# Attention loads of a fused attention and mixture-of-experts kernel tied to TensorE's position, with the strided values stored in 80 rows

## The chip, the cores and the metric

The kernel runs on one core of one Trainium2 chip. TensorE (PE), VectorE (DVE), ScalarE (ACT), GpSimd (POOL) and SyncE (SP) each work through their own instruction queue. Direct loads of this kernel are issued from SP's queue, indirect ones from POOL's, and all of them run on the core's 16 DMA engines. The metric is device time in microseconds (us) of one execution; lower is better.

## The reference

The reference is an attention layer whose output goes, token by token, through one of eight experts. Cut to what matters:

```
B, H, S, D = 8, 8, 576, 64            # heads 0-3 look at a local window, heads 4-7 at every 32nd key
rel = pos[:, None] - pos[None, :]
local   = (rel >= 0) & (rel < 32)
strided = (rel >= 0) & (pos[None, :] % 32 == pos[:, None] % 32)
scores = where(mask, q @ k.T / sqrt(D), -1e9)
x = (softmax(scores) @ v)             # -> N = 4608 tokens of 512 numbers
logits = x @ w_gate + modality_bias[modality_id];  e = argmax(logits)
out[token] = softmax(logits)[e] * (relu(x @ w1[e]) @ w2[e])       # w1: 512x1024, w2: 1024x512 per expert
```

All is float32.

## The kernel before

**Two stages.** The first stage computes the attention in 32 units; the second runs the experts' two matrix products over slots of 256 tokens that belong to one expert. The second stage starts while the routing of the last tokens is still being finished.

**Units.** A unit is either `Local` (one local head of two batches) or `Strided` (a pair of strided heads of one batch). They alternate: units 0, 2, 4 and so on are local, units 1, 3, 5 and so on strided, 16 of each. Eight units make a group of two batches, after which `finish_pair` turns the group's outputs round, computes its routing and scatters its token rows into a buffer in memory (`xd`).

**What a unit loads.** All of it is issued from SP's queue.
- Queries and keys: two loads of 296 KB (local, into `lqk`) or 288 KB (strided, into `sqk`). One fills the even rows of the tile and one the odd rows. Each kind has two tiles, used in turn, so a tile is free again once the scores of the unit four places earlier are done.
- Values of a local unit (`vv`, two tiles): the first seven local units (`SPREAD = 7`) load 317 KB in four pieces, `vb` twice, `ve` and `vf`, and two POOL copies of about 1 us each then spread them (`spread_values`). The other nine load 585 KB in two pieces from `vl`, without copies.
- Values of a strided unit (`vs`, two tiles): one load of 72 rows of 4 KB, 288 KB.

**The loop.** Iteration n of the loop at the end of the first stage calls, in this order: the query and key load of unit n+3, the value load of unit n-1, for even n `spread_values` of unit n-2, the scores of unit n, `turn` of unit n-2 (transposes of its weights on TensorE), the masks of unit n+1, and the products with the values (`values`) of unit n-3. Between these stand pieces of `finish_pair` (`pop`, `slow`).

**Who sets the order.** TensorE's instructions stand in the order of the program in this stage (`manual_schedule`). The queues of the other engines, SP's among them, are ordered by the framework's scheduler, which works with a cost model, unless an instruction is held in program order by `pin`. A load waits for what it needs: that its tile is free, and that the direct load eight places before it has landed, as the direct loads share eight semaphores in turn. The function `paced` adds one more wait to an instruction: for the TensorE instruction that `recent` names, which is the one recorded last in program order. It is used before for the scatters of the routing, for the early fetches of weights and tokens, and for two small copies.

## Time and profile before

| | |
|---|---|
| median of three runs | 599.7 us (595.32 to 600.47) |
| the profiled execution | 597.48 us, span of its instructions 595.4 us |
| mean granted TensorE clock in it | 0.977 of full speed |
| TensorE matmuls busy | 564.8 us, 95% of the span |
| first stage | from the start to about 158 us, when the first matmul of an expert runs |
| bytes moved by DMA | 100.57 MB, mean 169 GB/s |

In the rows of the profile an arrow points from what is read to what is written (`o<-vv,et`), `xN` counts records, and a bracket `[1.64 <-issue]` gives the time that the engine sat idle before and what ended it; "issue" stands where the engine waited for nothing that the profile shows. `PEld` rows are TensorE's loads of its stationary operand. `SPq` and `POOLq` rows are issues of DMAs. A window row gives, for a stretch of time, the busy microseconds and the records of each engine, then the granted TensorE clock, the mean busy share of the DMA engines and the GB/s that they moved.

### The profile page before, as it was taken

Reading aid. Unit: us, or ns where it says so; the run is one execution under the profiler, and the core shown is the slowest. Engines: PE = TensorE matmul, PEld = TensorE weight load, DVE = VectorE, ACT = ScalarE, POOL = GpSimd, SP = SyncE. Lnnn points to the kernel's source line nnn. Section 1 sums busy time; section 2 is a strip of 40 time slices with the busy share of each in tenths; the row PEclk is TensorE's granted clock in tenths of the full one; section 3 lists DMA queues with packets and bytes.
Section 4 is the critical chain, followed back from the end, with each engine's and each line's share of the span. In section 5 each row is a group of like instructions: output and inputs, shape, how many; then the busy total and the mean of one; then the engine's idle time right before and its main releaser. Section 6 shows DMA issues by size and latency. Waiting matters only on the chain.

```text
span 595.4 us, 15277 instructions
## 1 busy us (share of the span) xinstructions
PE 564.8 (95%) x6040; PEld 494.4 (83%) x6040; DVE 426.1 (72%) x1050; ACT 358.7 (60%) x739; POOL 244.7 (41%) x219
## 2 busy tenths in 40 slices
PE   6979888989998999999999999999999999999995
PEld 3767776767887989999899899999998998998984
DVE  6776662957969997767767777777777677677541
ACT  3455664657866566666666666665665666666641
POOL 1413240143757786642543533533534533332220
PEclk9789997989999999999999999999999999999998
DMA  8988895897788855955934823413403438200621
GB/s 275 250 220 217 250 344 189 276 341 258 262 215 210 259 164 164 236 184 129 250 119 125 248 98 74 108 36 73 109 21 87 109 119 252 71 16 22 244 91 38
DMA packets 66669, 100.57 MB, mean 169 GB/s; under 512 B 47775, under 2 KB 49055, under 8 KB 63008
## 3 DMA queue, kind: packets, MB, share of 16 engines
q0 software_dynamic: 19744, 58.57, 29.7%
q1 hardware_dynamic: 46560, 40.56, 27.0%
q8 instruction: 49, 0.80, 0.6%
q10 hardware_dynamic: 288, 0.41, 0.2%
q14 instruction: 28, 0.23, 0.1%
HBM read 121.74 MB, written 19.43 MB: 237 GB/s over the span
## 4 chain that ended last, share of the span: by engine, by line
PE 85%; issue 5%; DVE 4%; DMA 3%; ACT 2%; POOL 1%; SPq 0%; POOLq 0%; ACTq 0%
PE h L924 33%; PE o L938 32%; PE o L420 3%; PE s L380 3%; PE ot L520 3%; PE lg L571 2%; PE xs L217 2%; PE t L217 2%; PE ss L476 1%; PE xl L217 1%; PE ts L217 1%; DMA vv<-in_vb 1%; ACT wh L959 1%; DVE wl L960 1%; DMA lqk<-in_qkl 1%
## 5 line engine op out<-in xcount | busy, mean ns | idle before, releaser
L960 DVE TENSOR_TENSOR wl<-raw,wh 128x512 fp32r<-128x512 f32 x288 | 185.9, 686 | 85.0 <-ACT wh L959 84.9
L959 ACT CAST wh<-raw 128x512 fp32r<-128x512 f32 x288 | 164.0, 618 | 91.4 <-PE o L938 89.6
L924 PE MATMUL h<-xl,wh 128*128 128x256 f32 x576 | 162.1, 282 | 1.4 <-DVE xl L912 1.4
L924 PE MATMUL h<-xh,wh 128*128 128x256 f32 x576 | 163.0, 284 | 0.2 <-ACT xh L911 0.2
L924 PE MATMUL h<-xh,wl 128*128 128x256 f32 x576 | 162.8, 283 | 0.0
L811 POOL DMA_INDIRECT raw<-in_w,wi x72 | 92.7, 1287 | 162.4 <-DVE wl L960 154.1
L924 PEld LDWEIGHTS h<-xl,wh 128*128 128x128 f32 x576 | 108.8, 189 | 8.1 <-DVE xl L912 2.1
L938 PE MATMUL o<-wh,hh 128*128 128x512 f32 x288 | 114.6, 398 | 0.0
L924 PEld LDWEIGHTS h<-xh,wh 128*128 128x128 f32 x576 | 108.4, 189 | 7.1 <-issue 0.6
L938 PE MATMUL o<-wl,hh 128*128 128x512 f32 x288 | 113.6, 395 | 0.0
L938 PE MATMUL o<-wh,hl 128*128 128x512 f32 x288 | 112.2, 395 | 0.0
L924 PEld LDWEIGHTS h<-xh,wl 128*128 128x128 f32 x576 | 108.3, 188 | 0.9
L927 ACT ACTIVATE hh<-h 128x256 fp32r<-128x256 f32 x144 | 55.2, 384 | 55.0 <-PE h L924 52.7
L929 DVE SCALAR_TENSOR_TENSOR hl<-h,hh 128x256 fp32r<-128x256 f32 x144 | 60.3, 419 | 12.5 <-ACT hh L927 12.3
L646 POOL DMA_INDIRECT xd<-xt,posi x36 | 40.4, 1121 | 59.1 <-DVE sms L496 16.5
L938 PEld LDWEIGHTS o<-wh,hl 128*128 128x128 f32 x288 | 53.7, 188 | 11.8
L938 PEld LDWEIGHTS o<-wh,hh 128*128 128x128 f32 x288 | 54.3, 188 | 7.6
L938 PEld LDWEIGHTS o<-wl,hh 128*128 128x128 f32 x288 | 54.3, 189 | 5.8
L946 POOL DMA_INDIRECT out<-y,le x36 | 46.2, 1283 | 24.0 <-ACT y L945 16.1
L792 POOL DMA_INDIRECT fx<-xd,li x36 | 39.2, 1090 | 23.6 <-issue 8.5
L409 ACT COPY et<-t 64x512 f32<-64x512 f32 x32 | 18.5, 579 | 21.1 <-PE t L217 20.7
L420 PEld LDWEIGHTS o<-vv,et 128*64 128x64 f32 x512 | 19.0, 152 | 13.4 <-issue 10.1
(183 smaller groups left out, 687.9 us busy)
## 6 DMA issues: line engine op xcount, KB each, us to landing
lqk<-in_qkl SPq DMA_DIRECT2D x32, 296.0 KB
sqk<-in_qks SPq DMA_DIRECT2D x32, 288.0 KB
vv<-in_vl SPq DMA_DIRECT2D x9, 520.0 KB
vs<-in_vs SPq DMA_DIRECT2D x16, 288.0 KB
raw<-in_w,wi POOLq DMA_INDIRECT x72, 2.5
vv<-in_vb SPq DMA_DIRECT2D x7, 146.2 KB
vv<-in_vb SPq DMA_DIRECT2D x7, 130.0 KB
vv<-in_vl SPq DMA_DIRECT2D x9, 65.0 KB
```

What stands on the lines that cost most here:

```text
L217: recent[:] = [nc.tensor.transpose(dst, src, ident)]
L420: recent[:] = [nc.tensor.matmul(os[bb][64 * jj:64 * jj + 64, bb + k, :], et[:, 2 * (k // 2) + bb, 2 * (k % 2) + jj, :, :].rearrange("p g q ...
L646: scattered(bp, paced(nc.gpsimd.indirect_dma_start(xd[0:(bp + 1) * T2, :], IOA(ap=posi[:, i:i + 1], axis=0), xt[:, i, :], None)))
L792: yield xt, fetches(min(xrows // T2, NBP) - 1, nc.gpsimd.indirect_dma_start(xt[:, h, :], None, xd[0:xrows, :], IOA(ap=li[:, s, h:h + 1], a ...
L811: return nc.gpsimd.indirect_dma_start(raws[j].rearrange("p f c -> p (f c)"), None, a["w"], IOA(ap=wi[:, s, j:j + 1], axis=0), bounds_check ...
L924: recent[:] = [nc.tensor.matmul(hp, w[:, a1], x[:, c, :], start=(k == 0), stop=(k == 11))]
L927: nc.scalar.activation(hh[:], hp, AF.Relu)
L929: nc.vector.scalar_tensor_tensor(hl[:], hp, 0.0, hh.bitcast(F32), ALU.max, ALU.subtract)
L938: nc.tensor.matmul(os[h], hx[:, m], w[:, 512:1024], start=(f == 0 and i == 0), stop=(f == 7 and i == 2))
L946: outs.add(nc.gpsimd.indirect_dma_start(out, IOA(ap=le[:, h, 0:1], axis=0), y[:], None, bounds_check=NT - 1, oob_is_err=False))
L959: nc.scalar.copy(wh[:, c], raw[:, c])
L960: nc.vector.tensor_tensor(wl[:, c], raw[:, c], wh[:, c].bitcast(F32), ALU.subtract)
```

## The change

Four things are changed.

1. `load` of a unit issues one of its two query and key loads, chosen by `x`, where it issued both.
2. In the loop, for n of 1 and more, the first of the two (`x` = 0) is called at the head of iteration n and the second after the scores of unit n. Both go through `paced`: the first waits for the last recorded TensorE instruction of iteration n-1, the second for the last matmul of the scores of unit n. For that, local scores now also set `recent`, in their last four matmuls.
3. The value load of unit n-1 is called after `turn` of unit n-2 in iteration n, and goes through `paced` too: it waits for the last transpose of that `turn`. The value loads of the first two local and the first two strided units are held in program order by `pin` as before; only unit 0's is still called ahead of the scores.
4. The values of a strided unit are stored in 80 rows, eight of them zeros, and loaded into a tile of 80 rows (320 KB). The products read the first 72.

```
-    vs = np.ascontiguousarray(vs).reshape(B, 2, 72, 1024)
+    vs = np.concatenate([vs.reshape(B, 2, 72, 1024), np.zeros((B, 2, 8, 1024), np.float32)], axis=2)
...
-    def load_qk(t, nk, src):
+    def load_qk(t, nk, src, x):
         w = src.shape[1]
-        nc.sync.dma_start(t[0:P:2, nk:nk + w], src[0:64])
-        nc.sync.dma_start(t[1:P:2, 0:w], src[64:128])
+        if x:
+            return nc.sync.dma_start(t[1:P:2, 0:w], src[64:128])
+        return nc.sync.dma_start(t[0:P:2, nk:nk + w], src[0:64])
...
                 ins = nc.sync.dma_start(dst, src)      # Local.load_values; the same in Strided.load_values
                 if n < 2:
                     pin(ins)
+                else:
+                    paced(ins)
...
-                        nc.tensor.matmul(              # Local.scores, the last four matmuls
+                        recent[:] = [nc.tensor.matmul(
...
-            self.vs = lp.tile([72, 8, 2, D], F32, tag="vs", name=f"vs{n}")
+            self.vs = lp.tile([80, 8, 2, D], F32, tag="vs", name=f"vs{n}")
...
-                            vs[:, 4 * g2 + u, h, :],
+                            vs[0:72, 4 * g2 + u, h, :],
...
     for i in range(3):
-        units[i].load()
+        for x in range(2):
+            units[i].load(x)
...
     for n in range(nu + 3):
         if n + 3 < nu:
-            units[n + 3].load()
-        if 1 <= n <= nu:
-            units[n - 1].load_values()
+            if n:
+                paced(units[n + 3].load(0))
+            else:
+                for x in range(2):
+                    units[3].load(x)
+        if n == 1:
+            units[0].load_values()
         if 2 <= n <= nu + 1 and not n % 2:
             units[n - 2].spread_values()
         if n < nu:
             units[n].scores()
+            if n and n + 3 < nu:
+                paced(units[n + 3].load(1))
             if n % 2:
                 slow()
             pop(MIDS)
         if 2 <= n <= nu + 1:
             units[n - 2].turn()
+        if 2 <= n <= nu:
+            units[n - 1].load_values()
         slow()
```

On SP's queue this is what stands near its start, before the change; `lqk_84` and `lqk_85`, `sqk_86` and `sqk_87`, `vv_90` and `vv_91` are the pairs of tiles, and the sizes are rows by numbers per row.

```order
L326 DMA lqk_84<-in_qkl 64x1184
L327 DMA lqk_84<-in_qkl 64x1184
L353 DMA vv_90<-in_vb 32x1170
L353 DMA vv_90<-in_vb 32x1040
L353 DMA vv_90<-in_ve 64x130
L353 DMA vv_90<-in_vf 32x65
L326 DMA sqk_86<-in_qks 64x1152
L327 DMA sqk_86<-in_qks 64x1152
L463 DMA vs_243<-in_vs 72x1024
```

And the same place of SP's queue after it:

```order
L328 DMA lqk_84<-in_qkl 64x1184
L354 DMA vv_90<-in_vb 32x1170
L354 DMA vv_90<-in_vb 32x1040
L354 DMA vv_90<-in_ve 64x130
L354 DMA vv_90<-in_vf 32x65
L327 DMA lqk_84<-in_qkl 64x1184
L328 DMA sqk_86<-in_qks 64x1152
L327 DMA sqk_86<-in_qks 64x1152
L466 DMA vs_285<-in_vs 80x1024
```

The first unit's four value loads have moved ahead of one load of 296 KB.

In the middle of the stage, with the larger value loads, SP's queue before the change reads:

```order
L353 DMA vv_91<-in_vl 128x1040
L353 DMA vv_91<-in_vl 64x260
L326 DMA lqk_85<-in_qkl 64x1184
L327 DMA lqk_85<-in_qkl 64x1184
L463 DMA vs_1466<-in_vs 72x1024
L326 DMA sqk_87<-in_qks 64x1152
L327 DMA sqk_87<-in_qks 64x1152
L353 DMA vv_90<-in_vl 128x1040
L353 DMA vv_90<-in_vl 64x260
```

And after it:

```order
L328 DMA lqk_85<-in_qkl 64x1184
L327 DMA lqk_85<-in_qkl 64x1184
L354 DMA vv_91<-in_vl 128x1040
L354 DMA vv_91<-in_vl 64x260
L328 DMA sqk_87<-in_qks 64x1152
L327 DMA sqk_87<-in_qks 64x1152
L466 DMA vs_1506<-in_vs 80x1024
L328 DMA lqk_84<-in_qkl 64x1184
L327 DMA lqk_84<-in_qkl 64x1184
```

The value loads now stand behind the query and key loads of their iteration, where they stood ahead of them. TensorE's order in the first stage is the same in both kernels. On POOL the order of a few copies of the early stage against three small sums of the routing differs, and around the start of the second stage a few of the last group's scatters and of the weight fetches have changed places.

More of the change, by code (lines that the diff above doesn't have):

```diff
@@ L333, in __init__, with load @@
             self.bp, self.h, self.xt, self.n = bp, h, xt, 4 * bp + h
-        def load(self):
+        def load(self, x):
             n = self.n
             self.qk = lqk[n % 2]
-            load_qk(self.qk.rearrange("p x i q -> p (x i q)"), S + 32, a["qkl"][self.bp, self.h])
+            return load_qk(self.qk.rearrange("p x i q -> p (x i q)"), S + 32, a["qkl"][self.bp, self.h], x)
         def load_values(self):
@@ L390, in scores @@
                             start=False, stop=True, skip_group_check=True,
-                        )
+                        )]
                 mx = lp.tile([P, 5], F32, tag="mx", name=f"mx{n}{half}")[:, :gn]
@@ L453, in __init__, with load @@
             self.b, self.pr, self.xc, self.n = b, pr, xc, 2 * b + pr
-        def load(self):
+        def load(self, x):
             n = self.n
             self.qk = sqk[n % 2]
-            load_qk(self.qk.rearrange("p i q -> p (i q)"), S, a["qks"][self.b, self.pr])
+            return load_qk(self.qk.rearrange("p i q -> p (i q)"), S, a["qks"][self.b, self.pr], x)
         def load_values(self):
             n = self.n
-            self.vs = lp.tile([72, 8, 2, D], F32, tag="vs", name=f"vs{n}")
+            self.vs = lp.tile([80, 8, 2, D], F32, tag="vs", name=f"vs{n}")
             ins = nc.sync.dma_start(self.vs.rearrange("p g h d -> p (g h d)"), a["vs"][self.b, self.pr])
@@ L465, in load_values @@
                 pin(ins)
+            else:
+                paced(ins)
         def masks(self):
@@ L1046, in attention_moe @@
         if n + 3 < nu:
-            units[n + 3].load()
-        if 1 <= n <= nu:
-            units[n - 1].load_values()
+            if n:
+                paced(units[n + 3].load(0))
+            else:
+                for x in range(2):
+                    units[3].load(x)
+        if n == 1:
+            units[0].load_values()
         if 2 <= n <= nu + 1 and not n % 2:
```

## The prediction

> **What bounds the kernel now.** I read the strip of forty slices first, then windows, then TensorE's waits and its timeline. TensorE, its granted clock and the DMA engines in slices of 14.9 us:
>
> ```profile
> span 595.4 us, 15277 instructions
> PE   6979888989998999999999999999999999999995
> PEclk9789997989999999999999999999999999999998
> DMA  8988895897788855955934823413403438200621
> ```
>
> From slice 14 on TensorE is full and the DMA engines are not. All open time lies in the first ten slices, the attention stage, where the DMA engines are nearly full and the clock dips. The same in windows (after the length: busy time and records of PE, PEld, DVE, ACT and POOL; then clock, DMA share, GB/s):
>
> ```profile
> 0.00:135.00 135.00, 114.42 (x2756) 90.60 (x2757) 87.90 (x304) 71.87 (x167) 37.63 (x50) 0.91 0.86 263
> 15.00:30.00 15.00, 13.55 (x296) 11.02 (x296) 10.85 (x27) 6.00 (x13) 6.26 (x7) 0.77 0.95 250
> 44.72:50.54 5.82, 4.67 (x125) 4.00 (x126) 3.06 (x8) 3.93 (x9) 2.04 (x2) 1.00 0.97 233
> 50.54:72.20 21.66, 19.99 (x501) 16.43 (x500) 14.85 (x56) 14.70 (x36) 6.35 (x7) 1.00 0.85 238
> 72.20:91.06 18.86, 14.88 (x377) 12.52 (x377) 10.71 (x32) 10.22 (x24) 7.89 (x8) 0.90 0.94 323
> 91.06:110.02 18.96, 18.59 (x378) 14.22 (x379) 9.83 (x40) 10.25 (x25) 1.25 (x2) 0.83 0.61 196
> 110.02:115.10 5.08, 4.08 (x127) 3.35 (x127) 5.01 (x29) 2.39 (x7) 0.96 (x1) 1.00 1.02 285
> 115.10:121.07 5.97, 4.26 (x125) 3.43 (x125) 4.81 (x28) 4.22 (x10) 2.87 (x3) 1.00 0.86 310
> 200.00:300.00 100.00, 99.96 (x635) 90.16 (x634) 81.42 (x164) 62.96 (x124) 59.09 (x43) 1.00 0.71 199
> ```
>
> TensorE is idle for 20.6 of the first 135 us, and a mean clock of 0.91 takes up to 135 x 0.09 = 12 us more. In 200 to 300 us nothing is lost. What does TensorE wait for up to 160 us?
>
> ```profile
> PE o L420 <- issue: 7.4, 3, 4.0
> PE ss L476 <- issue: 3.6, 4, 1.4
> PE s L380 <- issue: 1.6, 1, 1.6
> PE s L387 <- issue: 0.8, 1, 0.8
> PE lg L571 <- issue: 0.7, 1, 0.7
> ```
>
> Ten waits, 14.1 us, for nothing that the profile shows. They do not look like waits for data:
>
> ```profile
> 86.40 0.68 PE L420 MATMUL o<-vv,et 128*64 128x65 f32 x15
> 91.06 1.24 PE L420 MATMUL o<-vv,et 128*64 128x65 f32 x17 [3.98 <-issue]
> 54.25 1.93 PE L571 MATMUL lg<-xc,wg_sb 128*32 128x256 f32 x32
> 93.86 3.63 PE L571 MATMUL lg<-xc,wg_sb 128*32 128x256 f32 x32
> ```
>
> The longest, 3.98 us, cuts a run of equal matmuls after 15 of 32. The windows above are cut where such waits end, and their matmul records are 125, 501, 377, 378, 127 and 125: multiples of 125, each with as many weight loads. So TensorE stops at a fixed period of its own instruction stream; I read it as the stream being fetched in blocks, and a block arriving late. After the long wait the clock is low: the same 32 matmuls take 3.63 us against 1.93. The blocks travel through the DMA engines as everything else, here up to 160 us (packets, MB, share):
>
> ```profile
> q1 hardware_dynamic: 10656, 31.64, 66.4%
> q8 instruction: 26, 0.43, 1.2%
> ```
>
> 0.43 MB in 26 packets is 16.5 KB each, next to 31.64 MB of loads from SP. The Trainium skill, "Runtime: NRT & Kernel Launch", section "Instruction fetch mechanics", says that an engine's instructions are refilled in blocks of 16 KiB (256 instructions) while the current one runs, and that crossing a boundary is mostly hidden. The size agrees (125 matmuls and 125 loads; 16.5 KB); the hiding does not, at ten boundaries of this stage. By the page's word alone the change would gain nothing.
>
> How long does a block take? From one late one to the next late one with nothing between, 5.08 to 5.97 us (the windows of one period); 125 records need only 4.08 to 4.67 us of PE. So a fetch misses by little, and cutting some 1.5 us of queue ahead of it would hide most of them.
>
> **The change part by part.** The sum is made against the profiled execution, 597.48 us (span 595.4 and 2.1 around it); the median shown, 599.7, is 0.4% above it.
>
> Loads let go one at a time (a). Before, they are issued as soon as a tile is free, several at once, up to eight under way. After, two loads and one value load leave per iteration at three points of TensorE's work. Bytes and rate stay the same, the queue in front of a block gets shorter. Bounds: 0 (DMA engines at 0.86 to 1.02 have a backlog whatever the order) to all 14.1 us. With misses of about a microsecond and one 4 us wait that sits in a pile of loads and scatters, I take half: -7.
>
> The clock (b). It is low behind the waits: 0.90 and 0.83 in the two windows around 91.06 are 18.86 x 0.10 + 18.96 x 0.17 = 5.1 us, of which the 32 matmuls are 1.7. Of the 12 us of the stage, 15 x 0.23 = 3.5 lie at 15 to 30 us, behind the wait for the first values (part c), and stay. Bounds 0 to -8; with half the late blocks gone I take a little under half, -3.5.
>
> Unit 0's values (c), one load of 296 KB earlier:
>
> ```profile
> 9.41 1.04 SPq L353 DMA_DIRECT2D vv<-in_vb  x2
> 15.90 1.04 POOL L360 COPY vv<-vv 32x1040 f32<-32x1040 f32 x1 [12.49 <-DMA vv<-in_vb]
> 18.04 2.00 PE L420 MATMUL o<-vv,et 128*64 128x65 f32 x30 [0.57 <-POOL vv L361]
> ```
>
> TensorE waits for these copies. 296 KB at 263 GB/s is 1.1 us; but there are other waits just before. Bounds 0 to -1.1; I take -0.4.
>
> Later values in the early stage (d). A value load now leaves behind `turn` of iteration n and is needed two iterations on, after the two POOL copies. Unit 12's (the last with copies) would leave at the `ts` transposes and is needed at `o`:
>
> ```profile
> 62.76 0.60 PE L217 MATMUL ts<-cf_sb,ens 128*72 128x128 f32 x4
> 69.50 1.03 PE L420 MATMUL o<-vv,et 128*64 128x65 f32 x27
> 31.49 0.82 SPq L353 DMA_DIRECT2D vv<-in_vb  x2
> 35.51 1.00 POOL L361 COPY vv<-vv 32x975 f32<-32x975 f32 x1 [6.60 <-DMA vv<-in_vb]
> 46.12 0.82 SPq L353 DMA_DIRECT2D vv<-in_vb  x2
> 52.48 1.00 POOL L361 COPY vv<-vv 32x975 f32<-32x975 f32 x1 [5.28 <-DMA vv<-in_vb]
> 54.31 1.16 POOL L360 COPY vv<-vv 32x1040 f32<-32x1040 f32 x1
> ```
>
> That leaves 69.50 - 63.36 = 6.1 us. Needed: 4.0 to 6.4 us from issue to the first copy (31.49 to 35.51, 46.12 to 52.48) and two copies, 2.2: 6.2 to 8.6. So 0.1 to 2.5 us of wait where iterations are short: three of the local units 4 to 12 (the others have the group's transposes between). With shorter queues the low end is nearer: 3 x 0.7 = +2. Behind a value load on SP the next iteration's query and key loads wait too; those are needed three iterations on, so nothing is charged.
>
> The last local unit (e). Iterations 32 and 33 have no scores, so its lead shrinks most:
>
> ```profile
> 143.10 0.93 SPq L353 DMA_DIRECT2D vv<-in_vl  x2
> 148.27 0.63 PE L217 MATMUL ts<-cf_sb,ens 128*72 128x128 f32 x4
> 152.63 1.15 PE L420 MATMUL o<-vv,et 128*64 128x65 f32 x32
> ```
>
> Issued at 143.10 now, it can leave at 148.9 and is needed at 152.63: 3.7 us for 585 KB that need 4.0 to 6.4 by the rows above. A wait of 0.3 to 2.7 us, at a place whose next product (unit 31's, with the last strided load right behind on SP) cannot fill it: +1.5. Expert matmuls that start just behind may hide part.
>
> Eighty rows (f). 16 x 32 KB more are 0.52 MB, 2.0 us of DMA time at 263 GB/s, spread over 150 us and beside TensorE: 0, bounds -1 to +2. The Trainium skill, "DMA: Bandwidth & Descriptors", section "Why a DMA increments its semaphore by 16 and not by 1", says that a direct load uses the largest number of engines up to 16 that divides its rows: by it 72 rows lie on 12 engines, six each, and 80 on 16, five each, which would speak for the padding. No view shows single engines. The sum doesn't use it.
>
> The products' count and sizes, the scores and the second stage stay; the few scatters and fetches that change places lie where TensorE is full: 0. `recent` set by local scores moves no scatter to another step: 0.
>
> Sum: -7 - 3.5 - 0.4 + 2 + 1.5 = -7.4, so 597.5 - 7.4 = **590 us**. What the attention stage gains the second stage gets whole, since TensorE is full from there to the tail.
>
> **The rivals.**
>
> All of it goes (A): no late block, clock full, no late values: -14.1 - 8 = 575 us. For it: the misses are small. Against: the scatters of 72 to 91 us stay, and a faster TensorE asks for the same bytes in less time.
>
> Throughput is the bound (B): the DMA engines are busy 0.86 of 135 us = 116 us as it is, TensorE 114. If blocks are late because the engines are full and not because loads come in bunches, each block waits as before, or a late load takes its place, and the time is 595 to 601. For it: 0.97 and 1.02 of DMA share in two windows of one period with moderate rates (233 and 285 GB/s). Against: 0.85 over the four periods up to 72.20, of which only the last ended late.
>
> Values arrive late (C), the slower end: the load's lead is cut to one pair of iterations while landing stays as it is. It decides at 6.1 - 2.2 = 3.9 us of landing for the early units: all rows seen are above that. At 6.4 us five early units wait 2.5 us each (12.5), the last one 2.7, and blocks are as late as before less some 4 us: 597.5 + 15 - 4 = 608; at the mean of 5.2 us, 1.3 x 5 + 1.5 - 4 gives 601. For it: DMA share 0.97 in the middle of that stage; each wait also lowers the clock. Against: the landings of before had bursts ahead of them. The Trainium skill, "DMA: Bandwidth & Descriptors", section "Rules for kernel authors", speaks for this one: issue a transfer early and wait for it late; the change does the contrary, and no trace here shows what that costs.
>
> That the change would not do what it says can be left out: SP's order shows the loads behind their steps.
>
> **How the numbers follow.** Forecast (584 to 595): 0.47. A (574 to 584): 0.11. B (595 to 601): 0.21. C (601 to 611): 0.21. A measurement tells about 1% from no change, here 6 us around 599.7. Faster than 593.7: nine tenths of the forecast and A, 0.53. Slower than 605.7: two thirds of C, 0.14. Within: 0.33. The range 581 to 605 leaves out about 0.06 of A below and 0.14 of C above. The forecast's own range is 584 to 595.
>
> **What would show it.** (a) right: the "issue" waits of TensorE up to 160 us fall from 14.1 to about 7 us, none as long as 3.98; wrong if they stay above 11. (b): mean clock up to 135 us at 0.94 or more. (c): `o` starts before 17.8 us. (d): new waits of `o` for the copies at L363/L364, 2 us in all; C if above 6. (e): `o` of the last local unit waits 1 to 2 us for `vv`. (f): no more than 0.5 MB in addition. The first expert matmul, at 158 us now, comes at about 150. The forecast falls if it comes at 155 or later, or if time is lost again behind 200 us.

## The result and the profile after

The changed kernel takes 599.3 us (median; 594.7 to 604.6) beside 597.8 us of the kernel before on the same chip: a ratio of 1.010 [1.006, 1.014]. A ratio counts only the runs within 1.5% of the fastest of their kernel, and as one run of the kernel before took 587.8 us, this first ratio has three of that kernel's 18 runs on its side; the two medians of all runs are only 0.3% apart. Two later measurements of the same kernel gave 0.999 [0.995, 1.003] and 1.001 [0.998, 1.005]. So the change makes no difference that can be measured, and the forecast gain of 7.4 us is not there. The profiled execution took 597.2 us, against 597.5 before.

The page of the changed kernel, with TensorE, its clock and the DMA engines in forty slices, and the bytes moved:

```profile
span 595.1 us, 15288 instructions
PE   7889889788899999999999999999999999999995
PEclk9799989899699999999999999999999999999999
DMA  8986898989697946864944823403404438200721
DMA packets 66861, 101.09 MB, mean 170 GB/s; under 512 B 47839, under 2 KB 49119, under 8 KB 63200
```

The early slices look better than before. There is a new hole, though: in slices 9 and 10 (134 to 164 us) TensorE is less busy than before, and in slice 10 the clock falls to 0.6. The same in windows, with the columns of the prediction; first the changed kernel:

```profile
0.00:135.00 135.00, 116.16 (x2862) 93.49 (x2866) 89.37 (x310) 77.41 (x177) 38.55 (x52) 0.95 0.85 267
135.00:165.00 30.00, 26.26 (x494) 22.89 (x493) 23.44 (x108) 20.18 (x47) 16.25 (x16) 0.83 0.80 270
200.00:300.00 100.00, 100.00 (x638) 90.62 (x637) 82.35 (x171) 63.52 (x126) 55.93 (x42) 1.00 0.70 195
```

And the kernel before in the window that the prediction did not show:

```profile
135.00:165.00 30.00, 28.57 (x599) 23.92 (x598) 25.83 (x114) 24.74 (x56) 16.84 (x16) 1.00 0.77 259
```

Up to 135 us the clock rose from 0.91 to 0.95, worth 135 x 0.04 = 5.4 us. From 135 to 165 us it fell from 1.00 to 0.83, which takes 30 x 0.17 = 5.1 us back. What TensorE waits for in the changed kernel, 5 to 160 us, the seven largest sums (total, times, longest):

```profile
PE o L423 <- issue: 4.0, 2, 3.2
PE ot L525 <- issue: 2.7, 1, 2.7
PE o L423 <- DMA vv<-in_vl: 2.4, 1, 2.4
PE ot L525 <- DVE xt L449: 2.3, 2, 1.7
PE o L423 <- POOL vv L364: 2.2, 3, 0.7
PE o L423 <- POOL vv L363: 2.1, 2, 1.2
PE ct L697 <- ACT xc L533: 1.5, 2, 0.8
```

In this pair of profiles the waits for instruction blocks, as the prediction reads "issue", are halved, 14.1 to 7.1 us (with 0.4 of `ct`, not among the rows shown). In their place stand waits for local values: 2.2 + 2.1 for the copies and 2.4 for the last load, 6.7 us where there were 1.3. Counted over all waits of TensorE from 5 to 165 us the sum is 20.1 us before and 20.3 after. So in this pair the waiting was exchanged, not removed. Whether the change did it, one pair of executions can't tell: e9 below shows how far the waits of an unchanged program differ.

One more wait is new here, that of `ot` for VectorE's `xt`. Most of it, 1.70 us, comes from an earlier scatter that still reads the tile `xt`:

```profile
132.45 0.82 DVE L449 TENSOR_TENSOR xt<-o,rs 128x256 f32<-128x256 f32 x2 [2.11 <-DMA xd<-xt,posi]
132.93 1.22 PE L525 MATMUL ot<-eb,vs 72*64 72x72 f32 x32 [1.70 <-DVE xt L449]
```

In the kernel before VectorE waits 0.26 us there and TensorE not at all: having got ahead, TensorE meets another transfer.

Where the lead of this execution was lost is seen on TensorE's timeline. The stretch runs from the count `ct` of the routing to the first expert matmul `h`; in the changed kernel:

```profile
142.83 0.17 PE L697 MATMUL ct<-cnt,cb_sb 128*128 128x24 bf16 x1 [0.76 <-ACT xc L533]
150.47 2.00 PE L423 MATMUL o<-vv,et 128*64 128x65 f32 x32 [2.42 <-DMA vv<-in_vl]
152.77 1.97 PE L217 MATMUL xt<-cf_sb,fx 128*128 128x128 f32 x8
154.66 2.19 PE L525 MATMUL ot<-eb,vs 72*64 72x72 f32 x32
156.78 2.96 PE L217 MATMUL xl<-cf_sb,xt 128*128 128x128 f32 x13
159.47 0.39 PE L929 MATMUL h<-xh,wh 128*128 128x256 f32 x1
```

The same stretch of the kernel before (its `o` at 152.63 is in the prediction):

```profile
148.00 0.17 PE L692 MATMUL ct<-cnt,cb_sb 128*128 128x24 bf16 x1 [0.75 <-ACT xc L528]
153.96 1.09 PE L217 MATMUL xt<-cf_sb,fx 128*128 128x128 f32 x8
155.43 1.22 PE L520 MATMUL ot<-eb,vs 72*64 72x72 f32 x32 [0.38 <-DVE wi L769]
156.58 1.64 PE L217 MATMUL xl<-cf_sb,xt 128*128 128x128 f32 x13
157.98 0.37 PE L924 MATMUL h<-xh,wh 128*128 128x256 f32 x1
```

At `ct` the changed kernel leads by 148.00 - 142.83 = 5.2 us; at the first `h` it is 1.5 us behind. The stretch takes 16.6 us instead of 10.0: 2.4 us are the wait for the last local values, and the products behind it run at half speed (2.00 for 1.15, 1.97 for 1.09, 2.19 for 1.22, 2.96 for 1.64 and 0.44 for 0.32 of five short ones), 4.1 us together.

### The profile page after: what moved, and what is told of

The parts are those of the page before. It is cut to its first block, busy times and chain, and to the rows that moved or that the text cites. A ratio compares the mean times of both kernels' runs of the same rounds, so it can differ in the third digit from the quotient of the medians.

```text
span 595.1 us, 15288 instructions
## 1 busy us (share of the span) xinstructions
PE 564.7 (95%) x6040; PEld 496.7 (83%) x6040; DVE 425.5 (72%) x1050; ACT 359.4 (60%) x739; POOL 238.7 (40%) x219
## 2 busy tenths in 40 slices
DMA packets 66861, 101.09 MB, mean 170 GB/s; under 512 B 47839, under 2 KB 49119, under 8 KB 63200
## 4 chain that ended last, share of the span: by engine, by line
PE 84%; DMA 6%; issue 4%; DVE 3%; ACT 1%; POOL 1%; SPq 0%; POOLq 0%; DVEq 0%; ACTq 0%
PE h L929 35%; PE o L943 33%; PE o L423 3%; PE ot L525 2%; PE s L383 2%; DMA xd<-xt,posi 2%; DMA vv<-in_vb 2%; PE xl L217 2%; PE ss L481 1%; PE t L217 1%; DMA vv<-in_vl 1%; PE xs L217 1%; PE ts L217 1%; DMA lqk<-in_qkl 1%; PE lg L576 1%
## 5 line engine op out<-in xcount | busy, mean ns | idle before, releaser
L816 POOL DMA_INDIRECT raw<-in_w,wi x72 | 88.7, 1232 | 161.6 <-DVE wl L965 151.8
L943 PEld LDWEIGHTS o<-wh,hl 128*128 128x128 f32 x288 | 53.6, 188 | 11.6
L951 POOL DMA_INDIRECT out<-y,le x36 | 49.2, 1366 | 28.6 <-ACT y L950 21.0
L651 POOL DMA_INDIRECT xd<-xt,posi x36 | 36.9, 1026 | 52.1 <-DVE inc L713 13.3
L797 POOL DMA_INDIRECT fx<-xd,li x36 | 37.8, 1051 | 27.5 <-DVE le L806 7.5
L423 PE MATMUL o<-vv,et 128*64 128x65 f32 x512 | 22.2, 238 | 10.8 <-issue 4.0
L423 PEld LDWEIGHTS o<-vv,et 128*64 128x64 f32 x512 | 19.0, 148 | 15.7 <-issue 7.1
```

The costliest lines, as they stand in the source:

```text
L423: recent[:] = [nc.tensor.matmul(os[bb][64 * jj:64 * jj + 64, bb + k, :], et[:, 2 * (k // 2) + bb, 2 * (k % 2) + jj, :, :].rearrange("p g q ...
L651: scattered(bp, paced(nc.gpsimd.indirect_dma_start(xd[0:(bp + 1) * T2, :], IOA(ap=posi[:, i:i + 1], axis=0), xt[:, i, :], None)))
L797: yield xt, fetches(min(xrows // T2, NBP) - 1, nc.gpsimd.indirect_dma_start(xt[:, h, :], None, xd[0:xrows, :], IOA(ap=li[:, s, h:h + 1], a ...
L816: return nc.gpsimd.indirect_dma_start(raws[j].rearrange("p f c -> p (f c)"), None, a["w"], IOA(ap=wi[:, s, j:j + 1], axis=0), bounds_check ...
L943: nc.tensor.matmul(os[h], hx[:, m], w[:, 512:1024], start=(f == 0 and i == 0), stop=(f == 7 and i == 2))
L951: outs.add(nc.gpsimd.indirect_dma_start(out, IOA(ap=le[:, h, 0:1], axis=0), y[:], None, bounds_check=NT - 1, oob_is_err=False))
```

## The experiments

All full-load kernels in one table, for the sections below. "First `h`" is the start of the first expert matmul; the waits are TensorE's from 5 to 165 us, in all, for instruction blocks, and for local values with their copies.

| kernel | ratio to before [95%] | first `h`, us | waits: all / blocks / values | clock 0-135, 135-165 |
|---|---|---|---|---|
| before | 1 | 158.0 | 20.1 / 14.1 / 1.3 | 0.91, 1.00 |
| changed | 1.010 [1.006, 1.014] | 159.5 | 20.3 / 7.1 / 6.7 | 0.95, 0.83 |
| e6, changed again | 0.999 [0.995, 1.003] | 157.0 | 19.5 / 9.1 / 5.7 | 0.97, 0.83 |
| e13, changed, third | 1.001 [0.998, 1.005] | 158.1 | 18.4 / 7.1 / 5.3 | 0.97, 0.83 |
| e2, 80 rows only | 1.001 [0.996, 1.005] | 154.9 | 16.9 / 12.6 / 0.7 | 0.94, 0.94 |
| e3, only queries and keys paced | 1.005 [0.999, 1.010] | 160.7 | 24.9 / 19.5 / 0 | 0.92, 1.00 |
| e4, only values moved and paced | 1.000 [0.995, 1.004] | 159.1 | 20.3 / 9.2 / 6.4 | 0.95, 0.94 |
| e5, changed with 72 rows (profile not used) | 1.003 [0.998, 1.008] | – | – | – |
| e1, changed, last two units' values early | 0.993 [0.989, 0.996] | 153.5 | 20.6 / 9.9 / 2.0 | 0.98, 1.00 |
| e11, the same again | 0.999 [0.995, 1.002] | 160.3 | 24.6 / 15.7 / 3.1 | 0.97, 1.00 |
| e15, the same, third | 1.002 [0.999, 1.005] | 158.9 | 22.3 / 14.7 / 2.8 | 0.99, 0.89 |
| e7, values first, last two early | 0.995 [0.991, 0.999] | 154.4 | 21.7 / 14.5 / 0 | 0.97, 1.00 |
| e14, the same again | 1.000 [0.996, 1.004] | 159.1 | 23.7 / 12.4 / 2.2 | 0.96, 1.00 |
| e9, before with only the last two units' values late | 1.000 [0.997, 1.004] | 160.6 | 19.9 / 7.1 / 4.5 | 0.96, 0.83 |
| e10, e4 with the last two early | 1.005 [1.003, 1.008] | 161.4 | 21.0 / 12.5 / 2.6 | 0.96, 0.89 |

### The parts apart

**e2**, the padding alone, in the kernel before:

```
+    vs = np.concatenate([vs.reshape(B, 2, 72, 1024), np.zeros((B, 2, 8, 1024), np.float32)], axis=2)
-            self.vs = lp.tile([72, 8, 2, D], F32, tag="vs", name=f"vs{n}")
+            self.vs = lp.tile([80, 8, 2, D], F32, tag="vs", name=f"vs{n}")
```

> The kernel before with nothing but the strided values in 80 rows. Theory 1: within 2 us of the kernel before (ratio 0.997 to 1.003), TensorE's waits without a shown cause about 14 us as before. Rival: the 0.5 MB more in a stage whose DMA engines are full cost 2 us or more (ratio above 1.003). Second rival: 80 rows lie better on the engines and the waits without a shown cause fall by 3 us or more.

Measured 1.001: the padding does nothing that can be measured. In this execution a lead in the first stage was lost again. Its first expert matmul comes 3.1 us earlier than before (154.88), yet the span ends 4.2 us later, since the second stage stops more than before:

```profile
185.32 0.73 PE L938 MATMUL o<-wh,hl 128*128 128x512 f32 x2 [3.01 <-DVE hl L929]
192.62 0.58 PE L924 MATMUL h<-xl,wh 128*128 128x256 f32 x1 [1.09 <-DVE xl L912]
```

**e3** paces only the query and key loads (values as before, 72 rows), **e4** only the values:

```
e3, on the kernel before:
-            units[n + 3].load()
+            if n:
+                paced(units[n + 3].load(0))
...
+            if n and n + 3 < nu:                     # behind the scores
+                paced(units[n + 3].load(1))
```

```
e4, on the changed kernel:
-            if n:
-                paced(units[n + 3].load(0))
-            else:
-                for x in range(2):
-                    units[3].load(x)
+            for x in range(2):
+                units[n + 3].load(x)
...
-            if n and n + 3 < nu:
-                paced(units[n + 3].load(1))
```

> Only the query and key loads are paced, one after the other; the value loads are issued as before the change and are not paced; 72 rows. Theory 1 (the pacing of query and key loads shortens the queue, the pacing of values only makes them late): TensorE's waits without a shown cause are 7 us or less up to 160 us, no wait for vv behind the first unit, ratio 0.985 to 0.995. Rival (it is the values' pacing that thins the queue): these waits stay above 11 us and the ratio is 0.997 to 1.003.

> Only the value loads are moved behind the transposes and paced; query and key loads are issued in pairs at the head of their iteration as before; 72 rows. Theory 1: the waits for late values come as in the changed kernel (about 4 us for the copies in the early stage, 2 us for the last local unit with the low clock behind it) while the waits without a shown cause stay above 10 us: ratio 1.005 to 1.015. Rival: the waits without a shown cause fall to 7 us as in the changed kernel, and the ratio is that of the changed kernel or better.

The waits for blocks are 19.5 us in e3 and 9.2 in e4, which has the changed kernel's pattern whole (6.4 us of waits for values). That speaks against the pacing of queries and keys as what shortens the waits for blocks, and for the later values; one profile of each doesn't show it, as e9 below has 7.1 and paces no load but those of the last two units' values. Neither kernel is faster (e3's six runs have a median of 604.1 us beside 599.2).

**e5** is the changed kernel with 72 rows, beside **e6**, the changed kernel unaltered, on one chip:

```
-    vs = np.concatenate([vs.reshape(B, 2, 72, 1024), np.zeros((B, 2, 8, 1024), np.float32)], axis=2)
+    vs = np.ascontiguousarray(vs).reshape(B, 2, 72, 1024)
```

> The changed kernel with 72 rows of strided values, so the pacing alone. The padding by itself measured 1.0006 of the kernel before. Theory 1 (the padding does nothing): the same as the changed kernel on the same chip, within 2 us, with a wait of 2 to 3 us for the last local values and the clock at half behind it. Rival: the padding matters once loads go one by one: 3 us or more above or below the changed kernel.

> The changed kernel once more, beside the variants of this call on one chip. Theory 1: ratio 1.000 to 1.012 to the kernel before, and again a wait of TensorE for the last local values of more than 1.5 us with the clock below 0.8 in the 10 us behind it. Rival (the wait was chance of one execution): no such wait in this profile.

1.003 [0.998, 1.008] and 0.999 [0.995, 1.003] overlap: no effect of the rows beside the pacing either. What e6 did show is that the 1.010 of the first measurement does not repeat. Its wait for the last local values is 0.5 us, where more than 1.5 was expected, and the clock is low behind 135 us all the same, here from 143.6 us on, behind a wait of 1.23 us for a block.

### The last local unit

**e1** lets the values of units 30 and 31 leave early and unpaced; **e9** does the contrary to the kernel before, and nothing else; **e10** is e4 with the edit of e1:

```
e1 on the changed kernel, e10 on e4:
-                else:                                # both kinds of values
+                elif n < 15:
                     paced(ins)
...
-        if n == 1:
-            units[0].load_values()
+        if n in (1, nu - 1, nu):
+            units[n - 1].load_values()
...
-        if 2 <= n <= nu:                             # behind turn
+        if 2 <= n < nu - 1:
             units[n - 1].load_values()
```

```
e9, on the kernel before:
+                elif n == 15:                        # both kinds of values
+                    paced(ins)
...
-        if 1 <= n <= nu:
+        if 1 <= n < nu - 1:
             units[n - 1].load_values()
...
+        if n in (nu - 1, nu):                        # behind turn
+            units[n - 1].load_values()
```

> The changed kernel, but the value loads of the last two units (30 and 31) are issued as soon as their tiles are free, at the head of their iteration and without the wait for TensorE. Theory 1: the changed kernel is 5 us ahead of the one before at 143 us and loses it where the last local values are late: the wait of 2.42 us for vv goes, the half clock behind it too (about 4 us), the first expert matmul runs at about 153 us instead of 159.5, and the time is 4 to 6 us below the changed kernel's, ratio to the kernel before 0.990 to 1.000. Theory 2: the start of the second stage is held by the weights, scatters and splits up to 190 us anyway: the wait goes, but the time stays within 1.5 us of the changed kernel's.

> The kernel before, with only the values of the last two units (30 and 31) loaded behind the transposes and paced, as the changed kernel has them. Theory 1 (the position of these two loads costs the changed kernel its lead): a wait for the last local values of 1 to 3 us, the clock under 0.8 for some 10 us behind it, ratio to the kernel before 1.004 to 1.012. Rival (the wait comes of TensorE being early, and the second stage absorbs it): no wait, or one without a change of the time, ratio 0.997 to 1.003.

> Only value loads are moved and paced, as in e4_values_paced, but those of the last two units are issued early and without it; query and key loads in pairs, 72 rows. Theory 1 (the pacing of the values is what keeps the waits short and the clock up, the tail what loses it): ratio 0.989 to 0.996, like e1_last_early. Rival (the query and key pacing is needed as well): 0.997 or above.

e1 seemed to settle it: no wait for the last values, clock 1.00 from 135 to 165 us, 0.993. e9 has the wait and the half speed, as foretold:

```profile
151.65 2.00 PE L422 MATMUL o<-vv,et 128*64 128x65 f32 x32 [2.31 <-DMA vv<-in_vl]
```

But its time is that of the kernel before, and e10, with the wait gone, is the slower of the two kernels that pace only the values.

e9 shows something else as well. Its instructions stand in the same order as the kernel before's on all five engines, and its first load that is held differently leaves at 145.15 us (143.10 before). Up to 135 us it is thus a second execution of the kernel before:

```profile
0.00:135.00 135.00, 116.66 (x2849) 92.53 (x2849) 87.60 (x310) 75.53 (x175) 38.48 (x52) 0.96 0.87 268
89.60 0.74 PE L422 MATMUL o<-vv,et 128*64 128x65 f32 x17 [1.58 <-issue]
```

The wait after 15 of 32 matmuls, 3.98 us in the prediction, is 1.58 here. The waits for blocks up to 135 us are 6.9 us against 14.1, the clock is 0.96 against 0.91, and `ct` comes at 144.26 against 148.00. So an unchanged program's execution differs by about as much as the changed kernel's profile did.

Repeats decided about the last loads:

> e1_last_early once more, on another chip: theory 1 (its gain is of the kernel, not of that chip's runs) 0.990 to 0.997, with no wait for the last local values.

> The changed kernel once more, beside the next two on one chip. Two measurements of it so far gave ratios of 1.010 and 0.999. Theory (exchange: the DMA engines are full in the attention stage, so that pacing puts waits for values in the place of waits for instruction blocks): waits for instructions and for values together 13 to 16 us up to 165 us, ratio 0.998 to 1.008. Rival (the change really costs 1%, and the second measurement was the odd one): ratio 1.007 or more.

> The changed kernel with the values of its last two attention units loaded early and unpaced, a third time (ratios 0.9929 and 0.9986 so far). Theory (the wait at the last local unit and the half clock behind it cost the changed kernel 3 to 6 us): ratio 0.993 to 0.999 and below that of the changed kernel on the same chip by 0.004 or more. Rival (the second stage's start has a gate of its own and swallows it): the same ratio as the changed kernel within 0.003.

e11 is e1 unaltered and gave 0.999; e15, a third time and beside the changed kernel (e13) on one chip, gave 1.002 where e13 gave 1.001. Taking the wait at the last local unit away is worth nothing that repeats. That wait itself is 2.42, 0.5 and 0.6 us in the three profiles of the changed kernel; in e13 too the half speed begins ahead of the last load, behind a wait for a block of 1.88 us. (e13's waits for blocks and values are 12.4 us together, a little under the 13 to 16 expected.)

e1, e11 and e15 run the changed kernel's program up to about 135 us, so that the profiles can be put together by program:

| profiles | blocks up to 135 us | clock 0-135 | `ct` to first `h`, us |
|---|---|---|---|
| program of the kernel before: before; e9 | 14.1; 6.9 | 0.91; 0.96 | 10.0; 16.4 |
| program of the changed kernel: changed; e6; e13; e1; e11; e15 | 6.7; 7.9; 5.0; 9.4; 13.7; 9.6 | 0.95; 0.97; 0.97; 0.98; 0.97; 0.99 | 16.6; 15.4; 16.9; 12.0; 13.8; 16.7 |

The last column is not the program's alone in its row: e9 has the last values late, and e1, e11 and e15 have them early. With values as before (before, e2 and e3) the stretch takes 10.0 to 10.7 us; with the last ones late it takes 15.4 to 16.9 in the changed kernel and e9, and 14.1 in e4.

**e7** asked for the values first in their iteration and for the two query and key loads behind the scores and behind the transposes, with the last two units' values early; **e14** is the same kernel again:

```
-                paced(units[n + 3].load(0))          # head of the iteration
+        if 1 <= n <= nu:
+            units[n - 1].load_values()               # head, paced
...
-                paced(units[n + 3].load(1))
+                paced(units[n + 3].load(0))          # behind the scores
...
-            units[n - 1].load_values()
+        if n and n + 3 < nu:
+            paced(units[n + 3].load(1))              # behind the transposes
```

> As e1_last_early (the last two units' values early), and in each iteration the value load goes first, paced by the end of the iteration before, the first query and key load after the scores, the second after the transposes: the same number of paced loads, in another order, the values some 2 us earlier. Theory 1 (the early-stage waits for the copies come from the position behind the transposes): these waits fall from 4.3 us to under 1.5 us, the waits without a shown cause stay at 7 to 10 us, and the ratio to the kernel before is 0.985 to 0.993. Rival (values are late because the DMA engines are full, wherever the load stands): 3 us or more of these waits remain and the ratio is that of e1_last_early, 0.993, or higher.

> The order with values first in their iteration and the last two units' values unpaced, once more (ratio 0.9947 before). Theory: no wait for the last local values, TensorE's clock at 1.00 from 135 to 165 us, ratio 0.993 to 0.998, and less than the changed kernel's of the same chip. Rival (the first measurement was chance, as that of the kernel with only the last values early seems to have been): ratio 0.998 to 1.002.

0.995, then 1.000. In e7 no local value was waited for and 14.5 us went to blocks, not the 7 to 10 expected; in e14 only the last local value was, for 2.2 us, where none was expected. None of the orders tried beats the kernel before in a way that holds.

### Fewer loads

**e8** takes loads out of the kernel before: the query and key loads of units 8 to 31, 24 x 2 x 0.29 = 14 MB, are not issued. **e17** is the same kernel, timed in rounds. On VectorE the framework's scheduler has put two rescalings (units 8 and 12) four instructions earlier; the other engines' work stands as before.

```
-        if n + 3 < nu:
+        if n + 3 < 8:
             units[n + 3].load()
+        elif n + 3 < nu:
+            u = units[n + 3]
+            u.qk = (lqk if isinstance(u, Local) else sqk)[u.n % 2]
```

> The kernel before, leaving out the query and key loads of units 8 to 31, whose scores are computed from what units 4 to 7 left in the tiles; TensorE's instructions are the same. Theory 1 (the waits without a shown cause are TensorE's own instructions arriving late behind the loads): those of the stretch in which loads are missing (from about 45 us on; 10.4 us of the 14.1 before) fall to under 1.5 us, the clock stays at 1.00 there, and the DMA share falls to about 0.6. Rival (they belong to TensorE's own queue): they stay near 10 us.

> The kernel before without the query and key loads of units 8 to 31 (they compute with what their buffers hold), a second time, now with an interval; one run of it took 586.6 us. Theory (the loads cost about 2% by what waits behind them, and the change cannot reach that): ratio 0.975 to 0.985, the first expert matmul before 150 us. Rival (that one run was a lucky one): ratio 0.99 or more.

e8 took 586.6 us in one run, e17 586.2 us, a ratio of 0.978 [0.974, 0.982]. The window of e8 up to 135 us:

```profile
0.00:135.00 135.00, 120.42 (x3137) 95.69 (x3139) 97.76 (x353) 82.16 (x193) 43.63 (x57) 1.00 0.60 186
```

And its waits for blocks from 45 to 165 us:

```profile
PE o L420 <- issue: 2.5, 3, 1.0
PE s L380 <- issue: 1.1, 1, 1.1
```

With the DMA share down from 0.86 to 0.60, the waits for blocks over 5 to 165 us fall from 14.1 to 4.6 us (3.1 in e17), all waits from 20.1 to 12.3 (12.2), and the first expert matmul comes at 142.95 (144.39). With e18 below this is the only edit whose waits in all lie clear of those of the others. The expected 1.5 us of waits for blocks behind 45 us is not reached: 3.6 remain.

**e12** is the changed kernel without the same loads, **e16** that with the last two units' values early:

```
-            if n:
+            if n + 3 >= 8:
+                u = units[n + 3]
+                u.qk = (lqk if isinstance(u, Local) else sqk)[u.n % 2]
+            elif n:
                 paced(units[n + 3].load(0))
...
-            if n and n + 3 < nu:
+            if n and n + 3 < 8:
                 paced(units[n + 3].load(1))
```

> The changed kernel, leaving out the query and key loads of units 8 to 31 as e8_fewer_loads did with the kernel before (the scores are computed from what units 4 to 7 left). Theory 1 (blocks and values are late because the DMA engines are full; the shorter lead of the values alone costs nothing): the waits for vv behind 45 us fall from 3.8 us or so to under 0.7 us, those without a shown cause stay at 3.6 us or less, and the span is within 3 us of e8_fewer_loads, 584.7. Rival (the lead of the values is too short even with room on the engines): 1.5 us or more of waits for vv remain behind 45 us, most of it at the last local unit.

> The changed kernel without the query and key loads of units 8 to 31 (they compute with the queries and keys of units 4 to 7 or what the buffers hold), as in the earlier kernel that took 597.4 us, and with the last two units' values early. Theory (the last local wait and the half clock behind it are what that kernel lost behind 143 us): no wait for the last values, clock 1.00 from 135 to 165 us, first expert matmul about 150 us where it was 158.7, and 588 to 592 us. Rival (a stop at the second stage's own gate takes it back): first expert matmul as early, but 595 us or more.

One run each: 597.4 and 596.7 us. So with the DMA engines at 0.56 the changed kernel is 10 us *slower* than the kernel before with the same loads. The last local wait (2.85 us in e12) is not why: e16 has none, starts its experts 4.3 us earlier, and is no faster beyond 1 us. That e12 waits 2.85 us there is what its rival named: the lead of the values can be too short with room on the engines too (a DMA share of 0.70 from 135 to 165 us). TensorE's waits in all are 17.0 us in e12 (4.5 for blocks) and 19.5 in e16 (6.2). Both traces fall behind e8 long before, most at one place near 45 us. There the product `ot` of the first group waits for VectorE, which has the chain of a strided unit's sums (`sms`, `ens`) ahead of the rescaling of a local unit's output (`rs`, `xt`). VectorE in e16:

```profile
41.01 0.45 DVE L499 TENSOR_REDUCE sms<-exs 128x16 f32<-128x288 f32 x1 [0.98 <-ACT exs L497]
41.50 1.05 DVE L500 TENSOR_SCALAR sms<-sms 128x16 f32<-128x16 f32 x1
42.88 1.01 DVE L503 TENSOR_TENSOR ens<-exs,sms 128x288 f32<-128x288 f32 x1
44.24 0.82 DVE L449 TENSOR_TENSOR xt<-o,rs 128x256 f32<-128x256 f32 x2
```

And TensorE in e16, released by that `xt` and slow behind it:

```profile
44.81 0.72 PE L525 MATMUL ot<-eb,vs 72*64 72x72 f32 x16 [1.77 <-DVE xt L449]
46.50 1.09 PE L217 MATMUL xl<-cf_sb,xt 128*128 128x128 f32 x4 [0.28 <-DVE ex L398]
```

This order is a by-product of the change that neither the diff nor the section on the change shows: VectorE's queue is ordered by the framework's scheduler, and with the loads moved it chose another order, here and around the routing (and, with loads left out, once more: e12 and e16 differ from the changed kernel in some further moves on VectorE and ScalarE, but not in the ones that follow). Near this place VectorE's queue before reads (with the line numbers of each kernel):

```
L442 TENSOR_SCALAR rs_854<-o_833 128x5
L443 RECIPROCAL rs_854<-rs_854 128x9
L494 TENSOR_REDUCE sms_813<-exs_810 128x16
L446 TENSOR_TENSOR xt_123<-o_832,rs_854 128x4x64
```

and after the change:

```
L499 TENSOR_REDUCE sms_808<-exs_805 128x16
L500 TENSOR_SCALAR sms_808<-sms_808 128x16
L501 RECIPROCAL sms_808<-sms_808 128x16
L503 TENSOR_TENSOR ens_812<-exs_805,sms_808 128x288
L445 TENSOR_SCALAR rs_854<-o_832 128x4
...
L449 TENSOR_TENSOR xt_123<-o_832,rs_854 128x4x64
```

**e18** puts the sums behind the rescaling at two places of the stage in e16:

```
-            nc.vector.tensor_reduce(sm[:], ex[:], AX.X, ALU.add)
+            sums[n] = nc.vector.tensor_reduce(sm[:], ex[:], AX.X, ALU.add)
...
+                if not bb and n in (3, 6):           # last: the rescaling `xt` of a local unit
+                    tc.add_manual_dep(sums[n + 1].ins, last.ins.name, ...)
```

> The changed kernel without those loads and with the last two units' values early (596.7 us in one run), with VectorE's order of the kernel before at two places of the attention stage: the sums of a strided unit's weights stand behind the first rescaling of a local unit's output, not ahead of it. Theory (the change's new order on VectorE is why it stays some 10 us behind the kernel before when the DMA engines are not full; the trace shows 1.8 us of wait of the product ot for that rescaling, and a lower clock behind it, 3.4 us in all): no wait of ot for it near 44 us, the first expert matmul 3 us earlier (about 151 us), ratio 0.985 to 0.99. Rival (the pacing of the early units costs it): ratio 0.993 or more, first expert matmul at 154 us or later.

584.5 us, 0.978 [0.973, 0.983], the same as the kernel before without those loads, with 12.8 us of waits in all (3.0 for blocks), though its instructions differ from e16's in those two places of VectorE's queue and in two moves of ScalarE's alone. TensorE's, SP's and GpSimd's orders are e16's. The stretch around the place in e16:

```profile
38.00:50.00 12.00, 9.67 (x206) 8.04 (x207) 8.13 (x21) 6.39 (x15) 4.20 (x5) 0.86 0.20 58
```

and in e18:

```profile
38.00:50.00 12.00, 12.00 (x290) 9.53 (x289) 9.89 (x29) 7.82 (x19) 6.05 (x7) 1.00 0.30 86
```

At the first place e18 gains 3.8 us on e16 (the masks `s` behind it start at 45.42 us in e18 and 49.97 in e16, those ahead at 37.92 and 38.72). Its first expert matmul comes at 143.33 against 154.41; the other 7 us are spread over the rest of the stage, and which of them come from the second place and which from the clock is not told apart. The theory's sum (0.985 to 0.99) was too small, its direction right. The changed kernel with all its loads and this order was not run. In it the first place shows no such wait: TensorE has stopped for the copies of `vv` just ahead, so that VectorE is done in time.

```profile
40.05 0.33 PE L423 MATMUL o<-vv,et 128*64 128x65 f32 x2 [1.24 <-POOL vv L363]
41.11 1.15 PE L423 MATMUL o<-vv,et 128*64 128x65 f32 x30 [0.72 <-POOL vv L364]
```

## Why the prediction was wrong, step by step

In the first pair of profiles most terms came nearly as forecast, and what was left out or too small made up for them: blocks -7.0, clock -5.4 up to 135 us and +5.1 behind it, values +5.4 and all other waits +1.8 are -0.1 us, where the two executions differ by 0.3. Against the repeats the largest term does not hold.

**The queue (a)**: -7.0 of waits for blocks against -7 forecast. By the sign set for it (about 7, none as long as 3.98; the longest is 3.20) it is right in this pair, by luck: the same program as before has 6.9 us up to 135 us in e9, and the changed program 5.0 to 13.7. The means, 10.5 of two and 8.7 of six profiles, are 2 us apart, and the scatter is larger than that. The reason given, a shorter queue by pacing, is not shown either: e3, with queries and keys paced, has 19.5.

**The clock (b)**: 0.95 up to 135 us, -5.4 against -3.5 in this pair; with 0.96 in e9 and 0.95 to 0.99 in the six profiles of the changed program a gain is possible but its size isn't shown.

**Unit 0's values (c)**: `o` starts at 15.78 (the 30 behind the copy) against 18.04: right by its sign, and more than the 0.4 charged, with the waits ahead of it shorter too; in e9, without the change, it is 16.75.

```profile
15.78 1.68 PE L423 MATMUL o<-vv,et 128*64 128x65 f32 x30 [0.72 <-POOL vv L364]
```

**Later values (d)**: 4.3 us of waits for copies against 1.3 before, +3.0 for +2; over the six profiles 2.0 to 5.2 against 1.3 and 2.2, which is +1.9 in the mean. The size is right, the place not: here they lie at units 0, 2 and 6, of which only the last was charged. The 6 us that mark rival C were not reached.

**The last local unit (e)**: the wait of 2.42 us is inside its bounds (0.3 to 2.7); its price was mis-sized. +1.5 was charged, and 2.4 + 4.1 = 6.5 us is what the stretch lost, because the clock halves behind it. "Expert matmuls just behind may hide part" was wrong: they wait for the same products. The page "DMA: Bandwidth & Descriptors" of the Trainium skill, section "Rules for kernel authors" (issue early, wait late), is borne out at this place by a lead of some 4 us that does not cover the landing.

```profile
144.09 0.88 SPq L354 DMA_DIRECT2D vv<-in_vl  x2
```

Issued at 144.09, this load lets `o` start at 150.47, 6.4 us later, the top of the range that the prediction had read for landings. In e6 and e13 the stretch is as long with waits of 0.5 and 0.6 us for these values, so that the late values are not all of its cause.

**Eighty rows (f)**: 0 was right (e2: 1.001; 101.09 MB moved against 100.57). That padding spreads the load over more engines, as the same page says in its section on semaphores, may be so; no time followed from it.

**The steps that failed** are the base of (a) and the price of (e). (a) took 14.1 us, the waits of a single execution, for a property of the kernel and charged half of it as the change's gain; the runs show 14.1 and 6.9 for one program and a mean that falls by 2 us at most. (e) charged 1.5 us for the way to the first expert matmul; it is 5.4 to 6.9 us longer in all three profiles of the changed kernel (15.4 to 16.9 us from `ct` on against 10.0). What lengthens it in each of them, late values or late blocks with the half clock behind, stays open; letting the last values leave early gives 12.0, 13.8 and 16.7 us and no faster kernel.

The outcome is that of rival B, "a late load takes its place, and the time is 595 to 601", which had a chance of 0.21; the profiled execution took 597.2 us. Its mark was in the prediction: the DMA engines busy 0.86 of a stage that TensorE fills to 0.85. One shortage behind the waits for blocks and for values is what the sums fit, though no run shows it for each wait. With all loads, TensorE waits 17 to 25 us of the first 165 in each of fourteen profiles, whatever the order (blocks and values together 11.6 to 19.5). Without 14 MB of them blocks and values together are 4.9 to 8.2 us in five profiles; the waits in all are 12.2 to 12.8 us in e8, e17 and e18, and 17.0 and 19.5 in e12 and e16, where other waits stand beside them. By the page "Runtime: NRT & Kernel Launch" of the Trainium skill, section "Instruction fetch mechanics" (crossings mostly hidden), the change should have gained nothing. The outcome agrees; the reason does not, since the crossings stay visible, 3 us even with the fewest loads.

A term was left out as well: VectorE's order. The prediction looked at SP's, TensorE's and GpSimd's queues and charged "the products' count and sizes, the scores and the second stage" at 0. In the variant without loads that by-product costs 12 us (e16, one run, to e18). What it costs in the changed kernel itself stays open.

"What the attention stage gains the second stage gets whole" holds nearly. In the profiles the span ends 436 to 442 us after the first expert matmul, but for e2 and e3, where 445 and 444 go by.

The 1% of the first measurement is no cost of the change: it rests on three runs of the kernel before, and the means of all 18 runs of each are 0.1% apart. e1's three ratios, 0.993, 0.999 and 1.002, differ by more than their intervals, and why stays open; differences below 1% between single measurements are not read here.

## What to carry to other kernels

Before a wait is charged as a gain, profile the unchanged kernel a second time: the same instructions waited 14.1 and 6.9 us. In this stage, with the DMA engines nearly full, no order of the loads lessened the waits in sum: add up all waits of the engine that should gain, not the kind one means to remove, and first leave loads out to see what the traffic costs at all (here 2.2%). After any edit that a scheduler sees, compare the order on every engine, those that the edit doesn't name too: two moved chains on VectorE were worth more, in one variant, than the edit itself. A difference below 1% is believed when it comes again.

## What the runs showed of the hardware

A wait of TensorE of about 2 us can be followed by half its speed, for up to some ten microseconds (2.42 us in the changed kernel, 2.31 in e9, 1.88 in e13: the next 32 matmuls of `o` take 2.00 or 1.54 instead of 1.15). It need not: in e14 a wait of 2.24 us is followed by full speed.

```profile
153.07 1.15 PE L423 MATMUL o<-vv,et 128*64 128x65 f32 x32 [2.24 <-DMA vv<-in_vl]
```

The Trainium skill, "TensorE: Matmul & The Clock Gate", section "Part 1: The HAM clock gate", puts the fall at an idle window of about 3.4 us that runs freely. That like waits have unlike ends would go with a free window; that waits this short suffice is seen here and not said in that section.

The waits for blocks are smaller with less traffic of data: up to 135 us 5.0 to 18.2 us in fourteen profiles at DMA shares of 0.82 to 0.88, and 1.9 to 4.6 us in five at 0.56 to 0.61. That fits blocks that share the way with the loads, as the prediction had read from their queue. How much a program waits for them differs by as much as 7 us from one execution to the next (before and e9).
